# The branch to the general path, moved ahead of the third token tile of the first expert

## The chip, the cores and the metric

The kernel runs on one core of a Trainium2 chip. The core has five engines, each with its own instruction stream: TensorE (PE in the profile, with PEld for its weight loads), VectorE (DVE), ScalarE (ACT), GpSimd (POOL) and SyncE (SP), which here issues most DMAs. They synchronise through semaphores. The metric is the device time of one execution in microseconds.

## The reference

The program is a retention layer (decayed causal attention, 4 batches x 8 heads x 576 positions x 64), then a layer of experts in which each token goes to its best expert alone, then a second layer of experts in which all experts are summed, weighted by a matrix P that is normalised over rows and columns eight times.

```
ret = (q @ k.T / 8) * decay;  x = (ret @ v) as 2304 tokens x 512
logits = x @ w_gate;  expert = argmax(logits);  g = softmax weight of that expert
x = g * (relu(x[expert's tokens] @ w1[expert]) @ w2[expert])        # 8 experts, 512 -> 1024 -> 512
P = exp(x @ w_gate2 - max), normalised 8 times
out = sum over e of P[:, e] * (relu(x @ w1b[e]) @ w2b[e])
```

How many tokens an expert of the first layer gets is known only at run time.

## The kernel before, in words

The retention and the gate go over the 2304 tokens in 18 tiles of 128. The gate counts the tokens of each expert. The first layer of experts is then a list of eight units, sorted by that count, with fixed room for 384, 352, 328, ... tokens (CAPS). Unit 0 takes the expert with the most tokens. If a count does not fit its room, a general path of loops (`anyhow`, L822) does the layer once more for whatever sizes there are. It hangs on one flag, entry [0, 4, 0] of the table `tab`. In the run profiled here the flag is 0, and the general path is jumped over. It has instructions on all five engines, so each of them reads the flag (`nc.values_load`, L829) and takes the branch (`tc.If`, L830) by itself. Where the branch is not taken, each engine does a few semaphore steps in place of what the general path would have counted.

The table `tab` (sorted experts, places, the flag) is worked out on DVE by `final_table` (L602), a generator of small steps. `table_step(n)` (L653) runs up to n of them; the calls are strewn between the matmuls of unit 0, so that the table's steps lie between other DVE work in the program. The step at L644 writes the flag, the one at L648 is the last. L629 writes the token numbers of units 1 to 7, and right behind it `gather(1)` (L665) has POOL issue three indirect DMAs (L671) that fetch unit 1's tokens.

A unit's tokens come as rows and are turned by PE (`gtrans`, L688: four transposes for one tile of 128 tokens); ACT copies the result as a high part HH (L690), DVE makes the low part HL from what is left (L691). Every product is done as three matmuls: high by high, high by low, low by high. Unit 0 is done by `first_unit` (L732), which differs from the others: it takes its three token tiles a = 0, 1, 2 one after another, since the last of them is gathered only when the whole gate is done. For each tile it goes over two halves f of the hidden layer, and for each half over i = 0, 1: `some` issues six matmuls (L697, L698, twice L700 among them). The third tile's transposes, `gtrans(0, 2)`, are issued in tile a = 1, half f = 1, after i = 0. `gemm2` then does the second product of the unit, and the next unit's `gtrans` lie in it. At the end of unit 0, L887 and L888 turn the list of its token numbers into `idsT`, then `anyhow()` stood, then `write(0)`.

The weights are loaded by SP in pieces of 512 KB (`load_more`, L229) into five buffers and split into a high part (ACT, L256) and a low part (DVE and POOL, both L233), which land in a ring of four slots. `keep_up` issues splits between matmuls; a load can go only when the splits of an earlier one are done.

The order of the instructions on an engine is the order in which the code is written: there is no scheduler. What stands in a queue behind an instruction that waits has to wait too.

Of the kernel before, what the change touches and what calls it, by code (L numbers as in the profile page):

```python
# [35 lines left out]
def kernel(  # L36
# [271 lines left out]
    with ExitStack() as at:  # L308
# [228 lines left out]
        def small(n, dt=F32):  # L537
            c = turn.get("s", 0)
            turn["s"] = c + n
            assert c + n <= 1024  # L540
            t = scr[:, c:c + n]
            return t if dt == F32 else t.bitcast(dt)
# [8 lines left out]
        def square(a, b, op):  # L551

            t = cube(E, E)
            nc.vector.tensor_tensor(t, a.unsqueeze(2).to_broadcast([128, E, E]), b.unsqueeze(1).to_broadcast([128, E, E]), op)
            return t
# [10 lines left out]
        def counts():  # L566
            c = small(E)
            nc.vector.tensor_tensor(c, base, cs[:, C_BASE:C_BASE + E], ALU.subtract)
            return c
# [32 lines left out]
        def final_table():  # L602
            turn["s"] = 0
            c = counts()
            key, rank, over, ov = small(E), small(E), small(E), small(1)
            yield
            nc.vector.scalar_tensor_tensor(key, c, 8.0, it8, ALU.mult, ALU.subtract)
            yield
            nc.vector.scalar_tensor_tensor(key, first, 65536.0, key, ALU.mult, ALU.add)
            yield  # L610
            m = square(key, key, ALU.is_lt)
            yield
            nc.vector.tensor_reduce(rank, m, AX.X, ALU.add)
            yield
            m = square(it8, rank, ALU.is_equal)
            yield
            ex = yield from total(m, it8)
            nc.vector.tensor_copy(tab[:, 0, 1:], ex[:, 1:])
            nc.vector.tensor_scalar(tab[:, 1, 1:], ex[:, 1:], float(N), None, ALU.mult)
            n_known[0] = len(raws)  # L620
            load_more()
            yield
            ids = small(3 * E * E).rearrange("p (u a e) -> p u a e", u=E, a=3)
            nc.vector.tensor_tensor(ids, listed[0].rearrange("p e a -> p a e").unsqueeze(1).to_broadcast([128, E, 3, E]),
                                    m.unsqueeze(2).to_broadcast([128, E, 3, E]), ALU.mult)
            yield
            nc.vector.tensor_reduce(rows.rearrange("p (u a) -> p u a", u=E), ids, AX.X, ALU.add)
            yield
            nc.vector.tensor_scalar(allid[:, 3:], rows[:, 3:], float(N), None, ALU.add)  # L629
            gather(1)  # L630
            yield
            cu = yield from total(m, c)
            n = small(E, I32)
            nc.vector.tensor_scalar(n, cu, 127.0, None, ALU.add)
            nc.vector.tensor_tensor(over, cu, cs[:, C_CAP:C_CAP + E], ALU.is_gt)
            yield
            nc.vector.tensor_reduce(ov, over, AX.X, ALU.max)
            nc.vector.tensor_scalar(tab[:, 3], n, 7, None, ALU.arith_shift_right)
            m = square(it8, it8, ALU.is_gt)
            yield  # L640
            r = yield from total(m, cu)
            nc.vector.tensor_tensor(ov, ov, short, ALU.max)
            yield
            nc.vector.tensor_copy(tab[:, 4, 0:1], ov)  # L644
            nc.vector.tensor_scalar(ov, ov, float(N), None, ALU.mult)
            nc.vector.tensor_copy(tab[:, 5], r)
            yield
            nc.vector.tensor_scalar(tab[:, 2], r, ov, None, ALU.max)  # L648
            yield

        table = []

        def table_step(n=5):  # L653
            for _ in range(n):
                if table and next(table[0], 0) == 0:
                    table.pop(0)
# [5 lines left out]
        def tokens(u, a):  # L662
            return min(128, CAPS[u] - 128 * a)

        def gather(u, a0=0, a1=3):  # L665
            if u >= E:
                return
            for a in range(a0, a1):
                n = tokens(u, a)
                x = temp(("p1", "u2", "u3")[a], name="xg")  # L670
                g = nc.gpsimd.indirect_dma_start(  # L671
                    out=x[0:n], out_offset=None, in_=xs[:],
                    in_offset=bass.IndirectOffsetOnAxis(ap=allid[0:n, 3 * u + a:3 * u + a + 1], axis=0),
                )
                arrives(0.73)
                G[u]["x"][a] = x
                if u == 0 and a < 2:
                    ahead.append(g)

        def gtrans(u, a):  # L680
            if u >= E:
                return
            n = tokens(u, a)
            x = G[u]["x"].pop(a)
            tick(0.436)
            p = bank_of("tr", (2, 3)).rearrange("p (k c) -> p k c", k=KB)[:, :, 0:n]
            for r in range(KB):
                nc.tensor.transpose(p[:, r, :], x[0:n, r * 128:(r + 1) * 128], ident[0:n, 0:n])  # L688
            t = slice(a * 128, a * 128 + n)
            nc.scalar.copy(HH[:, :, t], p)  # L690
            nc.vector.tensor_tensor(HL[:, :, t], p, HH[:, :, t].bitcast(F32), ALU.subtract)  # L691
# [40 lines left out]
        def first_unit():  # L732

            hidden(0)
            cc = take(), take()
            hh, hl = G[0]["h"]

            def htrans(a, f, h):
                tick(0.436)
                p = bank_of("tr", (2, 3)).rearrange("p (k c) -> p k c", k=4)  # L740
                for r in range(4):
                    nc.tensor.transpose(p[:, r, :], h[:, r * 128:(r + 1) * 128], ident)
                s, t = slice(f * 4, (f + 1) * 4), slice(a * 128, (a + 1) * 128)
                nc.scalar.copy(hh[:, s, t], p)
                nc.vector.tensor_tensor(hl[:, s, t], p, hh[:, s, t].bitcast(F32), ALU.subtract)

            wait = G[0]["late"] = []

            def late():
                if wait:  # L750
                    htrans(*wait.pop(0))

            for a in range(3):
                if a == 1:
                    gtrans(0, a)
                late()
                t = slice(a * 128, (a + 1) * 128)
                for f, c in enumerate(cc):
                    p = bank_of("h", (0, 1))
                    w = [x.rearrange("p (k f) -> p k f", k=KB) for x in (c.hi, c.lo)]  # L760
                    for i in range(2):
                        some(p, HH[:, :, t], HL[:, :, t], *w, (2 * i, 2 * i + 1), i == 0, i == 1)
                        for _ in range(2):
                            if a:
                                keep_up()
                            table_step(TS)
                        if i == 0:
                            if a == f == 1:
                                gtrans(0, 2)
                            if a > f or a == 2:  # L770
                                late()
                            yield
                    h = temp("c")
                    nc.scalar.activation(h, p, AF.Relu)
                    wait.append((a, f, h))
                    if a == 2:
                        release()
                    yield
            G[0]["late"] = late
# [87 lines left out]
        def unit_steps():  # L867
            for u in range(E):
                n = CAPS[u]
                if u == 0:  # L870
                    yield from first_unit()
                else:
                    gather(u + 1)
                    hidden(u)
                    yield from gemm1(u, 0, n)
                    yield from gemm1(u, 1, n)
                if u == E - 1:
                    return
                for f, d in gemm2(u):
                    if f == 0 and d:  # L880
                        gtrans(u + 1, d - 1)
                    elif u == f == d == 0:
                        G[0]["late"]()
                    yield
                if u == 0:
                    p = bank_of("tr", (2, 3))[0:3 * E, 0:128]
                    nc.tensor.transpose(p, rows, ident)  # L887
                    nc.vector.tensor_scalar(idsT, p, float(N), None, ALU.add)  # L888
                    anyhow()
                write(u)  # L890
                wrote(u)

# [1039 lines left out]
```

## Time and profile before

| what | value |
|---|---|
| median of 3 runs | 1841.89 us (1840.78 to 1845.59) |
| the profiled execution, its own time | 1840.57 us |
| its span, from first to last instruction | 1838.7 us |
| PE busy | 1803.2 us (98%) |
| DVE busy | 1235.5 us (67%) |
| ACT busy | 892.0 us (49%) |
| POOL busy | 567.3 us (31%) |

The profile is one execution on the chip. Busy is the time in which an engine executes; register, branch, semaphore and DMA-issuing instructions do not count as busy and are listed under the engine's queue (PEldq, DVEq, POOLq, SPq). A wait is the idle time of an engine before an instruction, with the one that released it. The change lies in the stretch from about 120 to 170 us, where unit 0 is computed.

### The profile page before, as it was taken

The numbers are of one execution on the slowest core, as the hardware profiler recorded it, in microseconds if no ns is written. First come the engines' busy times: TensorE is split into PE (matmuls) and PEld (weight loads), VectorE is DVE, ScalarE is ACT, GpSimd is POOL, SyncE is SP. The second block draws the span as 40 slices with busy tenths as digits, with TensorE's granted clock in tenths as the row PEclk, the third lists the DMA queues.
The fourth block names the chain that finished last, engine by engine and source line by source line (L and its number), as shares of the span: only waits on it lengthen the run. The fifth ranks groups of instructions, "written<-read, shape, count | busy, mean of one in ns | idle before, by whom it ended". The sixth has DMA issues, their size and how long they took to land.

```text
span 1838.7 us, 32928 instructions
## 1 busy us (share of the span) xinstructions
PE 1803.2 (98%) x12265; PEld 1721.5 (94%) x12265; DVE 1235.5 (67%) x2313; ACT 892.0 (49%) x1718; POOL 567.3 (31%) x582
## 2 busy tenths in 40 slices
PE   8889999999999999999999999999999999999998
PEld 7769999999899999999899999999999999999997
DVE  7984456547645554554467777778877777777778
ACT  2344456544434343434455555555655555555554
POOL 4455577532432323334311112111323111111212
PEclk9999999999999999999999999999999999999999
DMA  8755556564454556444755555655455545555540
GB/s 293 252 174 193 184 185 205 193 204 177 152 215 161 205 173 224 177 178 163 258 158 163 164 158 174 192 155 155 144 173 190 159 155 161 169 155 165 155 127 35
DMA packets 190455, 325.05 MB, mean 177 GB/s; under 512 B 20534, under 2 KB 93383, under 8 KB 190284
## 3 DMA queue, kind: packets, MB, share of 16 engines
q1 hardware_dynamic: 186716, 312.20, 52.0%
q0 software_dynamic: 3136, 9.95, 1.6%
q8 instruction: 99, 1.62, 0.4%
q10 hardware_dynamic: 432, 0.69, 0.1%
q14 instruction: 72, 0.59, 0.1%
HBM read 248.26 MB, written 74.53 MB: 176 GB/s over the span
## 4 chain that ended last, share of the span: by engine, by line
PE 85%; DVE 3%; issue 2%; ACT 1%; POOL 0%; DMA 0%; POOLq 0%; ACTq 0%; DVEq 0%
PE b L1507 8%; PE b L1508 8%; PE b L1509 8%; PE b L1655 8%; PE b L1656 8%; PE b L1654 8%; PE b L1154 5%; PE b L1155 5%; PE b L1156 5%; PE b L1224 4%; PE b L1226 4%; PE b L1225 4%; PE b L705 3%; PE b L706 3%; PE b L707 3%
## 5 line engine op out<-in xcount | busy, mean ns | idle before, releaser
L1655 PE MATMUL b<-wb,sq 128*128 128x256 f32 x1344 | 379.1, 282 | 1.1 <-DVE wb L233 1.1
L1654 PE MATMUL b<-wb,sq 128*128 128x256 f32 x1344 | 378.6, 282 | 0.9 <-DVE a L1676 0.9
L1656 PE MATMUL b<-wb,sq 128*128 128x256 f32 x1344 | 378.9, 282 | 0.4 <-DVE sq L233 0.4
L1655 PEld LDWEIGHTS b<-wb,sq 128*128 128x128 f32 x1344 | 254.7, 190 | 1.7 <-DVE wb L233 1.7
L1654 PEld LDWEIGHTS b<-wb,sq 128*128 128x128 f32 x1344 | 254.5, 189 | 1.8 <-issue 1.3
L1656 PEld LDWEIGHTS b<-wb,sq 128*128 128x128 f32 x1344 | 254.6, 189 | 0.6 <-DVE sq L233 0.6
L233 POOL TENSOR_TENSOR ring<-raw,ring 128x256 fp32r<-128x256 f32 x192 | 172.1, 908 | 262.7 <-ACT ring L256 210.4
L233 DVE TENSOR_TENSOR sq<-hq,sq 128x768 fp32r<-128x768 f32 x167 | 169.9, 1021 | 69.1 <-ACT sq L1600 68.9
L233 DVE TENSOR_TENSOR ring<-raw,ring 128x256 fp32r<-128x256 f32 (+1 forms) x256 | 153.1, 601 | 83.5 <-ACT ring L256 73.8
L1412 POOL TENSOR_TENSOR raw<-raw,raw 128x512 f32<-128x512 f32 x60 | 83.3, 1389 | 387.5 <-DVE wb L233 316.3
L1522 ACT ACTIVATE hq<-hq 128x384 f32<-128x384 f32 x144 | 75.6, 525 | 187.5 <-DVE hq L1519 187.1
L1507 PE MATMUL b<-ch,wa 128*128 128x384 f32 x448 | 152.0, 339 | 2.4 <-DVE hq L1519 0.9
L1224 PE MATMUL b<-ch,ring 128*128 128x384 f32 x448 | 153.2, 342 | 0.1
L1507 PE MATMUL b<-c,wa 128*128 128x384 f32 x448 | 151.6, 338 | 1.0 <-ACT u L1513 1.0
L1600 ACT CAST sq<-hq 128x768 fp32r<-128x768 f32 x167 | 137.7, 830 | 29.7 <-PE b L1655 25.7
L1509 PE MATMUL b<-c,wa 128*128 128x384 f32 x448 | 151.1, 337 | 0.0
L1509 PE MATMUL b<-ch,wa 128*128 128x384 f32 x448 | 151.1, 337 | 0.0
L1508 PE MATMUL b<-cl,wa 128*128 128x384 f32 x448 | 151.0, 337 | 0.0
L1508 PE MATMUL b<-c,wa 128*128 128x384 f32 x448 | 151.0, 337 | 0.0
L1226 PE MATMUL b<-ch,ring 128*128 128x384 f32 x448 | 151.0, 337 | 0.0
L1154 PE MATMUL b<-ring,HH 128*128 128x512 f32 x384 | 150.7, 393 | 0.0
L1225 PE MATMUL b<-cl,ring 128*128 128x384 f32 x448 | 150.6, 336 | 0.0
(257 smaller groups left out, 4359.1 us busy)
## 6 DMA issues: line engine op xcount, KB each, us to landing
wa<-w1s SPq DMA_DIRECT2D x192, 512.0 KB
raw<-in_moe_w_dram SPq DMA_DIRECT2D x128, 512.0 KB
w1s<-ring SPq DMA_DIRECT2D x64, 896.0 KB
raw<-in_moe_w_dram SPq DMA_DIRECT2D x106, 256.0 KB
wa<-w1s SPq DMA_DIRECT2D x64, 256.0 KB
sums<-in_moe_w_dram SPq DMA_DIRECT2D x22, 256.0 KB
kT<-in_kT_dram SPq DMA_DIRECT2D x18, 256.0 KB
qT<-in_qT_dram SPq DMA_DIRECT2D x18, 256.0 KB
```

What stands on the lines that cost most here:

```text
L233: eng.tensor_tensor(lo, x, hi.bitcast(F32), ALU.subtract)
L1154: nc.tensor.matmul(y[t], hh[:, s], w.hi[:, f0:f0 + 512], start=first, stop=False)
L1224: nc.tensor.matmul(ps, a, xh[:, r, :], start=first and r == 0, stop=False, skip_group_check=True)
L1225: nc.tensor.matmul(ps, a, xl[:, r, :], start=False, stop=False, skip_group_check=True)
L1226: nc.tensor.matmul(ps, b, xh[:, r, :], start=False, stop=r == 1, skip_group_check=True)
L1507: nc.tensor.matmul(ps, a, xh[:, r, :], start=first, stop=False, skip_group_check=True)
L1508: nc.tensor.matmul(ps, a, xl_[:, r, :], start=False, stop=False, skip_group_check=True)
L1509: nc.tensor.matmul(ps, b, xh[:, r, :], start=False, stop=r == 1, skip_group_check=True)
L1600: nc.scalar.copy(o.tile[0], src.tile)
L1654: nc.tensor.matmul(ps, hh[:, r, c], wh[:, r], start=st, stop=False, skip_group_check=True)
L1655: nc.tensor.matmul(ps, hh[:, r, c], wl[:, r], start=False, stop=False, skip_group_check=True)
L1656: nc.tensor.matmul(ps, hl[:, r, c], wh[:, r], start=False, stop=kh == 1 and r == 1, skip_group_check=True)
```

## The change

Three lines of code move. In `first_unit`, in tile a = 1, half f = 1, after i = 0, ahead of the third tile's transposes: all steps of the table that are left are issued at once (`table_step(99)`), then the general path with its branch (`anyhow()`). `gather(1)` leaves the table and is issued behind the transposes. At the end of unit 0 `anyhow()` is gone.

```
@@ final_table
             nc.vector.tensor_scalar(allid[:, 3:], rows[:, 3:], float(N), None, ALU.add)
-            gather(1)
             yield
@@ first_unit
                         if i == 0:
                             if a == f == 1:
+                                table_step(99)
+                                assert not table
+                                anyhow()
                                 gtrans(0, 2)
+                                gather(1)
                             if a > f or a == 2:
                                 late()
                             yield
@@ unit_steps
                     nc.vector.tensor_scalar(idsT, p, float(N), None, ALU.add)
-                    anyhow()
                 write(u)
```

The code behind it shifts by a few lines: L688 to L691 are L687 to L690 after, L829 and L830 are L833 and L834.

On PE, in unit 0, the third tile's transposes (L688; `xg` is the gathered tile, `ring` the split weights) stand between the matmuls of tile 1. Before:

```order
L697 MATMUL b_2243<-ring_79,HH 128x512
L698 MATMUL b_2243<-ring_79,HH 128x512
L700 MATMUL b_2243<-ring_79,HL 128x512 x2
L688 MATMUL b_2259<-cs,xg 128x128 x4
L697 MATMUL b_2243<-ring_79,HH 128x512
L698 MATMUL b_2243<-ring_79,HH 128x512
```

Now the load of the flag (L833) and the branch (L834) stand ahead of them, and the general path's 208 rows between the branch and its end:

```order
L696 MATMUL b_2237<-ring_79,HH 128x512
L697 MATMUL b_2237<-ring_79,HH 128x512
L699 MATMUL b_2237<-ring_79,HL 128x512 x2
L833 TENSOR_LOAD tab
L834 COMPARE_AND_BRANCH
...
L834 UNCONDITIONAL_BRANCH
L687 MATMUL b_3658<-cs,xg 128x128 x4
L696 MATMUL b_2237<-ring_79,HH 128x512
```

The transposes and all of the rest of unit 0 have moved behind the branch; what stood ahead of them is the same. The transposes write a bank of PSUM that the general path uses too, and in the new order they wait for a count of DVE that DVE reaches behind its own branch.

On DVE, the last steps of the table stood on both sides of the third tile's low part (L691). Before:

```order
L554 TENSOR_TENSOR sums<-cs 128x64
L560 TENSOR_TENSOR sums<-sums 128x64
L562 TENSOR_REDUCE sums<-sums 128x8
L691 TENSOR_TENSOR HL<-b_2259,HH 128x4x128
L642 TENSOR_TENSOR sums<-sums,short 128x1
L644 CAST tab<-sums 128x1
L645 TENSOR_SCALAR sums<-sums 128x1
L646 CAST tab<-sums 128x8
L648 TENSOR_SCALAR tab<-sums 128x8
```

Now they follow each other, and the branch stands behind them:

```order
L554 TENSOR_TENSOR sums<-cs 128x64
L560 TENSOR_TENSOR sums<-sums 128x64
L562 TENSOR_REDUCE sums<-sums 128x8
L641 TENSOR_TENSOR sums<-sums,short 128x1
L643 CAST tab<-sums 128x1
L644 TENSOR_SCALAR sums<-sums 128x1
L645 CAST tab<-sums 128x8
L647 TENSOR_SCALAR tab<-sums 128x8
L833 TENSOR_LOAD tab
L834 COMPARE_AND_BRANCH
```

Five small instructions have moved up by one place; L691 comes behind the branch.

On POOL, the gathers for unit 1 stood between two weight splits. Before:

```order
L233 TENSOR_TENSOR ring_71<-raw_65,ring_71 128x256 x2
L671 DMA xg<-xs,allid 128x512 x2
L671 DMA xg<-xs,allid 96x512
L233 TENSOR_TENSOR ring_78<-raw_66,ring_78 128x256 x2
```

Now POOL's branch stands ahead of them:

```order
L233 TENSOR_TENSOR ring_71<-raw_65,ring_71 128x256 x2
L833 TENSOR_LOAD tab
L834 COMPARE_AND_BRANCH
...
L834 UNCONDITIONAL_BRANCH
L670 DMA xg<-xs,allid 128x512 x2
L670 DMA xg<-xs,allid 96x512
L233 TENSOR_TENSOR ring_78<-raw_66,ring_78 128x256 x2
```

The gathers keep their place among the splits; the branch, six pairs of splits earlier than before, comes ahead of them. On SP six of the weight loads that stood ahead of the branch stand behind it, and on ACT the casts from the third tile's L690 on.

## Rows read from the trace of the kernel before

**Rows 1.** Page, busy time of an engine (share of the span) and instructions.
```profile
PE 1803.2 (98%) x12265; PEld 1721.5 (94%) x12265; DVE 1235.5 (67%) x2313; ACT 892.0 (49%) x1718; POOL 567.3 (31%) x582
```
**Rows 2.** Stretches: length; busy of PE, PEld, DVE, ACT, POOL; clock, DMA share, GB/s.
```profile
127.07:128.74 1.67, 0.00 (x1) 0.03 (x1) 1.67 (x3) 0.22 (x1) 1.67 (x3) 1.00 0.36 135
132.11:133.97 1.86, 0.00 (x1) 0.00 (x0) 1.72 (x10) 0.00 (x0) 1.55 (x2) 1.00 0.90 330
158.35:159.88 1.53, 0.01 (x1) 0.03 (x1) 0.28 (x1) 0.41 (x1) 0.00 (x0) 1.00 0.28 94
```
**Rows 3.** Timeline of PE: start, duration, instruction, [wait before it, its releaser].
```profile
126.45 0.61 PE L700 MATMUL b<-ring,HL 128*128 128x512 f32 x2
128.74 0.63 PE L688 MATMUL b<-cs,xg 128*128 128x128 f32 x4 [1.67 <-DMA xg<-xs,allid]
...
133.97 0.73 PE L700 MATMUL b<-ring,HL 128*128 128x512 f32 x2 [1.86 <-DVE sums L642]
...
144.32 0.60 PE L688 MATMUL b<-cs,xg 128*128 128x128 f32 x4
...
159.88 0.40 PE L705 MATMUL b<-HH,ring 128*128 128x352 f32 x1 [1.53 <-PEq L830]
```
**Rows 4.** Timeline of DVE, the table's last steps.
```profile
133.10 0.22 DVE L562 TENSOR_REDUCE sums<-sums 128x8 f32<-128x64 f32 x1
133.24 0.68 DVE L691 TENSOR_TENSOR HL<-b,HH 128x512 fp32r<-128x512 f32 x1
133.84 0.15 DVE L642 TENSOR_TENSOR sums<-sums,short 128x1 f32<-128x1 f32 x1
134.02 0.15 DVE L644 CAST tab<-sums 128x1 int32<-128x1 f32 x1
```
**Rows 5.** Line L829, the flag's load: ns min/median/max, first and last start (us).
```profile
L829 PEldq TENSOR_LOAD <-tab x1: 483/483/483, 155.2 to 155.2; - x1
...
L829 DVEq TENSOR_LOAD <-tab x1: 546/546/546, 158.4 to 158.4; - x1
```
**Rows 6.** Line L830, branch and semaphore steps behind it; SP's in two stretches.
```profile
L830 POOLq EVENT_SEMAPHORE  x5: 17/43/43, 160.4 to 160.7; - x5
...
L830 DVEq EVENT_SEMAPHORE  x2: 21/21/21, 163.3 to 163.4; - x2
L830 PEldq COMPARE_BRANCH  x1: 3826/3826/3826, 155.7 to 155.7; - x1
L830 POOLq COMPARE_BRANCH  x1: 58/58/58, 157.8 to 157.8; - x1
...
L830 DVEq COMPARE_BRANCH  x1: 72/72/72, 159.0 to 159.0; - x1
...
L830 SPq EVENT_SEMAPHORE  x5: 17/17/17, 163.6 to 163.9; - x5
...
L830 SPq EVENT_SEMAPHORE  x4: 17/17/17, 166.6 to 166.9; - x4
```
**Rows 7.** Stretches: the branch's new place, and DVE's jump before.
```profile
134.20:138.50 4.30, 4.30 (x24) 3.55 (x24) 2.34 (x7) 2.31 (x5) 1.64 (x3) 1.00 0.89 322
159.00:163.30 4.30, 3.42 (x21) 3.45 (x22) 0.00 (x0) 0.00 (x0) 1.04 (x2) 1.00 0.38 133
```
**Rows 8.** Stretches: a thin one of PE in the retention, and the next.
```profile
81.50:84.90 3.40, 1.55 (x21) 1.22 (x18) 3.08 (x15) 2.25 (x6) 0.90 (x3) 1.00 0.39 146
84.90:88.30 3.40, 3.40 (x35) 2.92 (x34) 2.74 (x11) 0.30 (x2) 2.66 (x3) 0.50 0.96 277
```
**Rows 9.** Timeline of POOL; last, gathers of L671 from issue to landing.
```profile
132.01 0.97 POOL L671 DMA_INDIRECT xg<-xs,allid  x1 [0.31 <-DVE sums L560]
133.29 0.95 POOL L671 DMA_INDIRECT xg<-xs,allid  x1 [0.31 <-issue]
...
137.82 4.58 POOL L233 TENSOR_TENSOR ring<-raw,ring 128x256 fp32r<-128x256 f32 x5 [2.35 <-ACT ring L256]
...
DMA to landing us min/median/max: 3.4/5.6/8.5
```

More of the change, by code (lines that the diff above doesn't have):

```diff
@@ L629, in final_table @@
             nc.vector.tensor_scalar(allid[:, 3:], rows[:, 3:], float(N), None, ALU.add)
-            gather(1)
             yield
@@ L768, in first_unit @@
                             if a == f == 1:
+                                table_step(99)
+                                assert not table
+                                anyhow()
                                 gtrans(0, 2)
+                                gather(1)
                             if a > f or a == 2:
@@ L888, in unit_steps @@
                     nc.vector.tensor_scalar(idsT, p, float(N), None, ALU.add)
-                    anyhow()
                 write(u)
```

## The prediction

> **What bounds the kernel now.** I read first the busy time of the engines: TensorE (PE) is busy 1803.2 us of the 1838.7 us span [rows 1], so only its idle time can be lost or won, and a change of order is worth what it does to PE's waits. Then I looked for PE's waits in the stretch that the diff touches, 127 to 160 us. The busy time by stretch shows three in which PE does nothing: 1.67 us, 1.86 us and 1.53 us, 5.06 us together [rows 2]. The timeline of PE says what ends each [rows 3]. At 128.74 the transposes of the third token tile (L688) start when the gathered rows have landed. At 133.97 the first matmul with the low part HL starts, which VectorE (DVE) wrote late (L691 ends at 133.92 [rows 4]; the row names DVE's next step). At 159.88 PE comes out of the branch to the general path (PEq L830). Nothing else in this stretch idles PE. The timeline of DVE then explains the second wait and dates the flag on which the branch decides: DVE is at work on weight splits and on the table; its last table steps are L562 at 133.10, then the tile's HL (L691) at 133.24, then L642 at 133.84 and L644 at 134.02, which writes the flag and takes 0.15 us [rows 4]. Last I read the flag's load and the branch engine by engine [rows 5, 6].
>
> **The change, part by part.** *The table in one go.* Five DVE steps (L642 to L648) move ahead of one, L691. L642 takes the place of L691 at 133.24, and L644 follows 0.18 us later, so the flag stands at 133.24 + 0.18 + 0.15 = 133.57 us, 0.6 us earlier than before [rows 4]. It can't be much earlier, since all other table steps stood ahead of L691 already, and nothing that DVE does between 127 and 133 us waits for PE.
>
> *The branch, on PE.* It moves from the end of the unit to a place that PE reaches at 127.07 us (the last matmul before it starts at 126.45 [rows 3]; its wait starts at 127.07 [rows 2]). There PE must wait for the flag, read it, jump, and only then do the transposes. In the trace PE's sequencer reads the flag at 155.2 and the first matmul behind the branch starts at 159.88: 4.68 us, of which the jump itself is 3.83 and the rest 0.85 [rows 3, 5, 6]. The array lost only 1.53 us of this, because the sequencer was some 3 us ahead of it: work queued before the branch still ran until 158.35, when the array's wait starts [rows 2]. This cover is gone in the new place: the sequencer stands at the flag while the array runs dry.
>
> *How long a jump takes there.* After its compare-and-branch at 159.0 DVE goes on at 163.3, 4.3 us later; POOL needed 2.6 us (157.8 to 160.4) [rows 6]. There PE jumped at 155.7, POOL at 157.8, DVE at 159.0; now all five engines are released by one write and jump together, and in that stretch the DMA engines carry 322 GB/s at a share of 0.89, against 133 GB/s at 0.38 while DVE jumped [rows 7]. So for PE: 3.83 us if company costs nothing, 3.83 + (4.3 - 2.6) = 5.5 us if it costs PE what it cost DVE beside POOL. I take 5.0, nearer to the upper end because more engines and more traffic meet. PE goes on at 133.57 + 0.85 + 5.0 = 139.4 us. A second leg reaches the same place: the transposes behind the branch write a bank that the general path uses too, so they wait for DVE to be through its own branch; from flag to the end of its jump DVE needs 5.0 us (158.4 to 163.4 [rows 5, 6]), 138.6 us here. Even a cheap jump of PE would thus not be used.
>
> *Sum of the waits.* New wait: 139.4 - 127.07 = 12.3 us. What it replaces: the landing of the gather (long over by 139), the wait for HL (DVE has nothing else to do by then, L691 takes 0.68 us [rows 4], and PE needs HL only 133.97 - 1.86 - 128.74 = 3.4 us after the transposes start), and the old branch: 5.06 us. Net +7.3 us. The bounds: +4.9, if both legs jump in POOL's 2.6 us (PE goes on at 137.0), and +10.0, if one of them stands still a second time as SP did (2.7 us, under the rivals).
>
> *The clock.* In the trace PE waited 1.67 and 1.86 us here and its granted clock stayed full, 2.4 GHz [rows 2]. But at 81.5 to 84.9 us, where it was busy 1.55 of 3.4 us, the granted clock of the next 3.4 us was 0.50, the lower level of 1.2 GHz [rows 8]. A wait of 12 us is emptier than either, so I expect the lower level when PE goes on, for a stretch like that one: 3.4 us at half speed cost 1.7 us. Bounds: 0, as after the short waits, and 3.4, two such stretches. The Trainium skill ("TensorE: Matmul & The Clock Gate", Part 1: The HAM clock gate) holds that half speed is the resting state and only activity lifts it. By this rule the 1.7 us are due; by the row of the 1.86 us wait nothing would be, and the sum would end at 1847.9. I side with the rule because the rows at 81.5 us do.
>
> *What moves past POOL and SP.* The three gathers for the next unit now stand behind POOL's branch. Before they began at 132.01 [rows 9]; now POOL is through at about 138 to 139, issues them 1.3 us apart, and the longest landing is 8.5 us [rows 9], so the first is in by 149. PE needs it 144.32 - 128.74 - 1.86 = 13.7 us after it goes on [rows 3], at 153. Hidden, with 4 us to spare. POOL's weight splits, the first at 137.82 before [rows 9], are due 137.82 - 1.86 - 128.74 = 7.2 us after PE goes on, at 146.6; POOL is free at 143. Six weight loads move behind SP's branch; each waits for splits of that kind, so they lose nothing. ScalarE's (ACT's) casts fall back with PE. I cost all this at 0; if the cover failed, a late gather would cost up to 1 or 2 us.
>
> Sum, against the profiled execution's own 1840.57 us (1.9 us more than its span): +7.3 + 1.7 = +9.0, 1849.6 us. The median of the three runs shown is 1841.89, 1.3 us above the profiled one, the best of them 1840.78; I predict 1850.0.
>
> **The rivals.** *A hidden jump (the other side: not slower).* While PE stands at the flag it could have the target's code at hand; then it goes on at 133.57 + 0.85 = 134.4, the wait is 7.4 us, and the kernel takes 1840.6 + 2.3 = 1842.9, no change. For it: the array paid only 1.53 us for the old branch [rows 2]. Against it: that was queued work, and DVE, with nothing queued, stood still for 4.3 us [rows 6]; DVE's leg must be short too. It decides below a jump of about 3.2 us, where the loss falls under 5.5 us. For a gain, PE would have to go on before 127.07 + 5.06 = 132.1, ahead of the flag itself. The Trainium skill ("Runtime: NRT & Kernel Launch", Instruction fetch mechanics) says that a jump out of the code already fetched waits for a DMA. By this rule the hidden jump falls away; no row shows an engine that stood waiting ahead of its branch.
>
> *A second fetch.* Behind its jump SP did five semaphore steps from 163.6 to 163.9 and the other four from 166.6 [rows 6]: it stood still again for 2.7 us. If PE's new place, or DVE's or ScalarE's that PE needs next, has such a break, add 2.7: 1849.6 + 2.7 = 1852.3, and with a longer stretch at half clock about 1853.5. Nothing in the trace tells which engine it hits; it hit one of five.
>
> *The clock stays up.* Sum without 1.7: 1847.9 with my jump, 1846.7 with PE's 3.83.
>
> **How the numbers follow.** The forecast has 0.57 (own range 1848 to 1852.5), the second fetch 0.20, the clock that stays 0.12, the hidden jump 0.11. A measurement of this kernel tells about 0.3%, 5.5 us, from no change. Slower by more: the forecast, the second fetch and about half of the third, 0.84. Within: the other half and most of the hidden jump, 0.14. Faster: 0.02. The range takes the bounds of the sum: 1840.57 + 4.9 = 1845.5 below, and above 1840.57 + 10.0 + 3.4 + 1.3 = 1855.3, rounded to 1855.5; it leaves the hidden jump out.
>
> **What would show it.** Right: one wait of PE of about 12 us from 127 us, ended by the branch, no wait for HL and none at the unit's end, a granted clock of 0.5 behind it; DVE's flag write ending near 133.6; everything behind shifted alike. Wrong: PE going on before 137, the flag much earlier or later, the clock at full, or a new wait for the gather at the next unit's first transposes.

## The result, and the profile after

| | median | lowest to highest | runs |
|---|---|---|---|
| before | 1841.93 us | 1840.78 to 1845.59 | 4 |
| after | 1852.18 us | 1851.43 to 1853.67 | 4 |

The ratio is 1.0053, 95% interval 1.0038 to 1.0068: 10.25 us slower, which is more than the 5.5 us that can be told from no change. The forecast was 1850.0 us, its range 1845.5 to 1855.5. The profiled execution after took 1852.76 us, its span 1851.0 us, 12.3 us more than before's span.

The page's busy times are those of [rows 1] but for a few us; the loss is idle time of PE.

```profile
PE 1806.0 (98%) x12265; PEld 1724.6 (93%) x12265; DVE 1236.3 (67%) x2313; ACT 892.2 (48%) x1718; POOL 566.0 (31%) x582
```

The timeline of PE answers to [rows 3] (start, duration, instruction, wait before it with its releaser):

```profile
128.89 0.61 PE L699 MATMUL b<-ring,HL 128*128 128x512 f32 x2
143.91 1.09 PE L687 MATMUL b<-cs,xg 128*128 128x128 f32 x4 [14.41 <-PEq L834]
...
160.07 0.60 PE L687 MATMUL b<-cs,xg 128*128 128x128 f32 x4
...
173.83 0.27 PE L891 MATMUL b<-cs,rows 128*24 128x128 f32 x1
173.86 0.41 PE L704 MATMUL b<-HH,ring 128*128 128x352 f32 x1
```

Three waits have become one of 14.41 us ahead of the third tile's transposes, ended by the branch. The wait for HL is gone, the next unit's transposes at 160.07 wait for nothing, and at the unit's end (173.86) PE goes straight on. By stretches (columns as in [rows 2]), the wait as a whole, two parts of it, and what comes behind it:

```profile
129.51:143.91 14.40, 0.00 (x0) 0.03 (x1) 6.35 (x23) 0.21 (x1) 4.99 (x7) 0.61 0.63 204
136.40:141.00 4.60, 0.00 (x0) 0.00 (x0) 0.00 (x0) 0.00 (x0) 0.00 (x0) 0.50 0.90 309
...
143.91:149.70 5.79, 5.79 (x18) 4.81 (x19) 1.32 (x2) 1.77 (x3) 2.84 (x3) 0.50 0.34 97
149.70:153.00 3.30, 3.30 (x17) 2.73 (x17) 0.76 (x2) 1.20 (x3) 0.00 (x0) 1.00 0.21 63
98.50:101.90 3.40, 3.40 (x21) 2.77 (x16) 2.61 (x9) 1.12 (x3) 2.11 (x3) 0.50 0.73 218
```

DVE works 6.35 us of the 14.40 and then stops. From 136.40 to 141.00 no engine computes, while the DMA engines are busy at a share of 0.90 (0.81 over the 7.03 us of PE's jump, dated below). Behind the wait the granted clock is 0.50 for 5.79 us, then 1.00 again. (The last row is a stretch of the retention, for the accounts below.) DVE's timeline dates the flag, as [rows 4] did:

```profile
135.30 0.22 DVE L562 TENSOR_REDUCE sums<-sums 128x8 f32<-128x64 f32 x1
135.44 0.15 DVE L641 TENSOR_TENSOR sums<-sums,short 128x1 f32<-128x1 f32 x1
135.62 0.15 DVE L643 CAST tab<-sums 128x1 int32<-128x1 f32 x1
...
145.66 0.69 DVE L690 TENSOR_TENSOR HL<-b,HH 128x512 fp32r<-128x512 f32 x1 [9.42 <-ACT HH L689]
```

Then the flag's load and the branch, engine by engine (ns min/median/max, first to last start), as [rows 5, 6]:

```profile
L833 PEldq TENSOR_LOAD <-tab x1: 491/491/491, 135.8 to 135.8; - x1
L834 SPq EVENT_SEMAPHORE  x9: 17/17/17, 143.8 to 144.4; - x9
L834 POOLq EVENT_SEMAPHORE  x5: 17/42/43, 144.0 to 144.3; - x5
L834 DVEq EVENT_SEMAPHORE  x2: 21/21/21, 143.6 to 143.8; - x2
L834 POOLq COMPARE_BRANCH  x1: 58/58/58, 136.4 to 136.4; - x1
L834 PEldq COMPARE_BRANCH  x1: 7033/7033/7033, 136.4 to 136.4; - x1
L834 DVEq COMPARE_BRANCH  x1: 72/72/72, 136.6 to 136.6; - x1
```

The flag stands at 135.62 + 0.15 = 135.77. PE jumps at 136.4 for 7.03 us; POOL goes on at 144.0 (7.6 us) and DVE at 143.6 (7.0). The five jump together and are through together. Last, the DMA queues while they jump, 136.4 to 143.5 us (packets, MB, share of 16 engines), and SP's issues:

```profile
q1 hardware_dynamic: 924, 1.77, 78.0%
q14 instruction: 4, 0.03, 1.3%
q8 instruction: 1, 0.02, 0.9%
```

```profile
132.78 2.90 SPq L229 DMA_DIRECT2D raw<-in_moe_w_dram  x5
```

Five weight loads of 512 KB, issued up to 0.7 us before the branch, fill the DMA engines, and the few packets of instructions share these engines with them. PE's code comes as one packet of 16 KB on q8: before's trace has one at 157.12, the only instruction packet between PE's branch at 155.7 and POOL's at 157.8. After has it at 141.06, 4.6 us behind PE's branch, and PE is through 2.4 us later. The DMA view of 141.0 to 141.5 us:

```profile
q8 instruction: 1, 0.02, 13.0%
```

**Where the 12.3 us went.** I paired the matmuls of the two traces by their place in the program. After is 2.45 us late already where it reaches the place (129.51 against 127.07). In this execution the retention has one more stretch at half clock, from 98.5, beside that of [rows 8]; about 1.1 us came with it, 1.0 us had gathered in small steps before it, and the rest came behind it. The code of the retention is the same in both, so I put the 2.45 us down to the scatter of executions and not to the change. Then, in us: +12.74 for the wait (14.41 in place of 1.67), +2.6 for the half clock behind it, -1.92 for the wait for HL, -1.87 for the old branch, -0.42 just behind that, -1.25 for several small waits later. Sum 12.3; without the retention's part 9.9, against 10.25 between the medians.

### The profile page after: what moved, and what is told of

The parts are those of the page before. It is cut to its first block, busy times and chain, and to the rows that moved or that the text cites. A ratio compares the mean times of both kernels' runs of the same rounds, so it can differ in the third digit from the quotient of the medians.

```text
span 1851.0 us, 32923 instructions
## 1 busy us (share of the span) xinstructions
PE 1806.0 (98%) x12265; PEld 1724.6 (93%) x12265; DVE 1236.3 (67%) x2313; ACT 892.2 (48%) x1718; POOL 566.0 (31%) x582
## 4 chain that ended last, share of the span: by engine, by line
PE 86%; DVE 2%; issue 2%; ACT 1%; DMA 0%; POOL 0%; POOLq 0%; ACTq 0%; DVEq 0%
PE b L1510 8%; PE b L1511 8%; PE b L1512 8%; PE b L1658 8%; PE b L1659 8%; PE b L1657 8%; PE b L1157 5%; PE b L1158 5%; PE b L1159 5%; PE b L1227 4%; PE b L1229 4%; PE b L1228 4%; PE b L704 4%; PE b L706 4%; PE b L705 4%
```

## The experiments

Two theories of the 7 us jump. T, traffic: the code that an engine jumps to comes by DMA, and comes late because it stands among five weight loads. C, company: five engines fetch at once, and that costs. Each run is compared with the kernel before on the same chip (median 1843.42 us for e1 to e4, 1843.14 us for e5 to e8).

**e1: the loads behind the branch.** After, with the five loads taken out of the table and issued behind the branch.

```
@@ final_table
-            n_known[0] = len(raws)
-            load_more()
             yield
@@ first_unit
                                 anyhow()
+                                n_known[0] = len(raws)
+                                load_more()
                                 gtrans(0, 2)
```

> The changed kernel, with one thing more: the five weight loads that the table releases (and their order to SP) are issued behind the branch instead of ahead of it, so that nothing else moves on the DMA engines while the five engines jump. Theory T (the fetch of the code behind the jump stands in line behind the weight loads): PE's jump falls from 7.0 us to between 2.6 and 4.3 us, the wait at the third tile from 14.4 to about 11 us, the other engines' jumps likewise; the time falls by about 3 us against the changed kernel, to some 1849 us. Theory C (five fetches at once are slow, whatever else moves): the jump stays at 7 us and the time at 1852 us. Under both the clock is at half behind the wait.

Measured: 1849.36 us, ratio 1.0033 (1.0021 to 1.0044). The branch, the timeline of PE, and two stretches of e1:

```profile
L834 POOLq EVENT_SEMAPHORE  x5: 17/42/43, 138.1 to 138.4; - x5
...
L834 DVEq EVENT_SEMAPHORE  x2: 21/21/21, 138.5 to 138.6; - x2
L834 POOLq COMPARE_BRANCH  x1: 58/58/58, 134.4 to 134.4; - x1
L834 PEldq COMPARE_BRANCH  x1: 3373/3373/3373, 134.4 to 134.4; - x1
L834 DVEq COMPARE_BRANCH  x1: 72/72/72, 134.7 to 134.7; - x1
```

```profile
138.64 1.09 PE L685 MATMUL b<-cs,xg 128*128 128x128 f32 x4 [11.38 <-DVEq L834]
```

```profile
134.40:138.50 4.10, 0.00 (x0) 0.00 (x0) 0.00 (x0) 0.00 (x0) 0.00 (x0) 0.50 0.05 12
138.64:143.20 4.56, 4.56 (x15) 3.87 (x16) 0.69 (x1) 1.21 (x3) 2.83 (x3) 0.50 0.48 155
```

All five engines still jump together, at a DMA share of 0.05 instead of 0.90, and PE's jump is 3.37 us instead of 7.03. So T holds for PE, and C falls for PE: in e4 and e8 below, where the engines jump one after another, its jump takes 3.37 and 3.49 us. Company is not free for every engine: POOL's jump takes 3.7 us here (134.4 to 138.1) and took 2.6 in the old place [rows 6], and SP's takes 3.9 here and 2.5 to 2.6 in e4 and e8, where it is the first to jump. Why stays open. PE's packet now starts 1.0 us behind its branch, and PE is again through 2.4 us later. The DMA view of e1, 135.0 to 135.5 us:

```profile
q8 instruction: 1, 0.02, 12.5%
```

It took as long as after's (1.00 against 1.04 us). What the loads lengthen is therefore the time until the packet starts. With the DMA share over PE's jump, it is 1.0 us in e1, e2, e4 and e8 (0.05 to 0.11), 1.4 to 1.7 in before, e5 and e7 (0.33 to 0.44), 3.5 in e3 (0.88), and 4.6 and 4.8 in after and e6 (0.81 and 0.87). In all of them PE is through 2.4 to 2.7 us after the packet's start.

PE is through its own branch at 137.8, but goes on at 138.64, when DVE is through its: the second leg of the prediction, seen on its own. The wait is 3.0 us shorter than after's; the half clock stays. The interval of the ratio overlaps with after's, so the 3 us are read from the wait and not from the times.

**e2: a filler ahead of the branch.** e1, with 40 matmuls of no use queued on PE ahead of the flag's load, so that PE is busy while it would wait.

```
                                 table_step(99)
                                 assert not table
+                                fp = bank(7)
+                                for _ in range(40):
+                                    nc.tensor.matmul(fp, HH[:, 0, 0:128], w[0][:, 0], start=True, stop=True)
                                 anyhow()
```

> As the kernel before it in this list (loads behind the branch), with 40 matmuls of 512 columns into a bank that nobody reads, ahead of the branch on PE: 9.3 us of array work that lies inside the wait. Theory 'the clock falls because the array is empty': under T the empty time left is about 2 us, the granted clock stays at 1.0 and the 2.6 us that the half clock cost behind the wait are gone, time some 2.6 us under the kernel without the matmuls. Rival (the matmuls hold up the flag's load, since PE's sequencer has to get past them): PE goes on later by up to 3 us, and nothing is gained.

Measured: 1847.27 us, ratio 1.0023 (1.0013 to 1.0033). Timeline of PE and the stretch behind the branch in e2:

```profile
127.76 9.23 PE L771 MATMUL b<-ring,HH 128*128 128x512 f32 x40
139.35 0.63 PE L685 MATMUL b<-cs,xg 128*128 128x128 f32 x4 [2.37 <-DVEq L837]
```

```profile
139.35:144.00 4.65, 4.65 (x27) 3.95 (x28) 1.38 (x2) 2.00 (x4) 2.84 (x3) 1.00 0.46 151
```

PE reaches the place at 127.76 and goes on 11.6 us later, as late as in e1 (11.4), so the filler stands in nobody's way. The clock stays at 1.00, and in 4.65 us PE does 27 instructions where e1 did 15 in 4.56. At e2's pace those 15 take 4.65 * 15 / 27 = 2.6 us, so e1 lost about 2 us; its median is 2.1 us longer. That the clock falls behind this wait because PE is idle, and what it costs, is thereby shown, though the intervals of the two ratios overlap.

**e3: traffic at the old place.** Before, with four loads of 384 KB that nobody reads, issued as unit 0 ends.

```
+                    if u == 0 and f == d == 1:
+                        for j, tg in enumerate(("x00", "x01", "x10", "x11")):
+                            junk = xc_p.tile([128, 2, 384], F32, tag=tg, name="junk")
...
+                            nc.sync.dma_start(out=junk, in_=w21[j][0:256, 0:384].rearrange("(k p) f -> p k f", p=128))
```

> The kernel before, branch in its old place, with four loads of 384 KB into buffers that nobody uses yet, issued from about 155 us on, so that the DMA engines are busy while PE jumps (each engine still jumps at its own time as before). Theory T: PE's jump grows from 3.8 us to 6 or 7, its wait at the unit's end from 1.5 to 4 or 5 us, time +3 us. Theory C: PE's jump stays at 3.8 us, its wait at 1.5 us, time as before.

Measured: 1844.58 us, ratio 1.0003 (0.9994 to 1.0013). The branch, PE's timeline and stretches of e3:

```profile
L830 PEldq COMPARE_BRANCH  x1: 5932/5932/5932, 157.0 to 157.0; - x1
```

```profile
163.24 0.63 PE L705 MATMUL b<-HH,ring 128*128 128x352 f32 x1 [3.64 <-PEq L830]
```

```profile
157.00:163.00 6.00, 2.60 (x16) 2.25 (x14) 0.75 (x3) 1.48 (x3) 1.62 (x2) 0.94 0.88 253
163.24:169.00 5.76, 5.76 (x20) 5.76 (x21) 1.36 (x3) 1.59 (x3) 2.10 (x2) 0.50 0.66 215
```

PE jumps alone here, 2.1 us ahead of the next engine, and still takes 5.93 us at a DMA share of 0.88; undisturbed it took 3.83 [rows 6], and 4.23 and 4.31 in e5 and e7, which leave the old branch alone. This shows T from the other side. The wait grows from 1.53 to 3.64 us, less than the 4 to 5 that I expected, and in this execution half clock follows. The 3 us that I expected in the time did not come: 1.2 us more in the medians can't be told from nothing, and the interval ends at 2.4 us.

**e4 and e8: the flag known.** The branch in its new place hangs on a constant 0, so the general path is left out. The table's steps, with the next unit's gathers and the five loads among them, are held until the branch is issued and run behind it. In e4 the constant is a new tile, in e8 it lies in a cell that existed.

```
...
-            flag = nc.values_load(tab[0:1, 4, 0:1], min_val=0, max_val=1)
+            flag = nc.values_load(zero[0:1, 0:1], min_val=0, max_val=1)                  # e4
+            flag = nc.values_load(gap.bitcast(I32)[0:1, 0:1], min_val=0, max_val=1)      # e8
```

> The branch in its new place, but it hangs on a constant 0 written at the start, and the table's steps, with the next unit's gathers in them, run behind the branch. It leaves out that the general path is taken when counts don't fit. Theory (of the 14.4 us, 6.3 are the wait for the flag and 7 the jump, lengthened by the loads that the table releases): no engine waits for the flag, no load is in flight, the engines jump at 124 to 128 us in 2.6 to 4.3 us each, and PE's wait at the third tile is 2 to 5 us instead of 14.4; the waits for HL and at the unit's end are gone; time 1840 to 1843 us. Rival: the later table makes the next unit's gathers late (they are needed 13.7 us behind the transposes), and 2 to 5 us come back there: 1844 to 1846 us.

> Once more the branch in its new place on a constant 0, table and gathers behind it, but the constant lies in a cell that the kernel has already, so that no buffer moves to another address. It leaves out that the general path is taken when counts don't fit. In the run with a cell of its own, PE lost 5 us evenly between 440 and 1600 us, far from the change. Theory (that loss came with the new cell, not with the branch): it is gone, PE's wait at the third tile is about 5 us again, ended by DVE's branch, the waits for HL and at the unit's end are gone, time 1842 to 1844 us. Rival (the loss belongs to the branch or to chance): 1847 us or more again.

Measured: e4 1847.99 us, ratio 1.0029 (1.0018 to 1.004); e8 1841.74 us, ratio 0.9995 (0.9986 to 1.0004). e4's PE waits 4.64 us in the new place, e8's 3.98. Branch and PE's timeline in e8:

```profile
L835 DVEq EVENT_SEMAPHORE  x2: 21/21/21, 135.8 to 135.9; - x2
...
L835 PEldq COMPARE_BRANCH  x1: 3493/3493/3493, 128.7 to 128.7; - x1
...
L835 DVEq COMPARE_BRANCH  x1: 72/72/72, 132.3 to 132.3; - x1
```

```profile
135.88 1.09 PE L690 MATMUL b<-cs,xg 128*128 128x128 f32 x4 [3.98 <-DVEq L835]
```

```profile
135.88:141.90 6.02, 6.02 (x19) 4.95 (x20) 2.60 (x10) 1.77 (x3) 0.85 (x2) 0.50 0.01 3
```

PE's jump is over at 132.2, nearly all of it hidden behind work that was queued ahead of the branch, yet PE goes on at 135.88 because DVE jumps from 132.3 to 135.8. This cover is that of the old branch and not the hidden jump of the rivals, which was to come from code at hand. DVE's leg takes most of it back, and half clock follows the wait here too. Still, one wait of 4 us in place of three of 5.06 makes no measurable difference in the times. In e8 the flag is not late, and the five loads are not in flight: the two together make the loss, not the place alone, and e1 gives the loads' share, 3.0 us of the wait.

e4 missed its expected 1840 to 1843 by 5 us, and its wait does not explain them. Paired by matmuls, e4 falls behind by 5.2 us between 440 and 1600 us, where the code is the same: there the new 4-byte tile had moved the buffers behind it by 32 bytes (HH from 58720 to 58752). The same 7225 matmuls, far behind the change, in before, in e4 and in e8:

```profile
440.19:1600.04 1159.85, 1156.00 (x7225) 1111.34 (x7224) 776.07 (x1238) 572.30 (x1078) 293.29 (x288) 1.00 0.54 176
```

```profile
445.84:1610.89 1165.05, 1161.94 (x7225) 1115.87 (x7224) 774.32 (x1238) 572.69 (x1078) 293.42 (x289) 1.00 0.54 175
```

```profile
445.73:1605.00 1159.27, 1155.56 (x7225) 1111.21 (x7224) 774.25 (x1238) 572.30 (x1078) 294.11 (x289) 1.00 0.54 176
```

At full clock e4 takes 1165.05 us for them where before takes 1159.85, and e8, with the addresses kept, 1159.27. The loss is uneven: from 400 to 1800 us the mean time from one matmul to the next goes from 228.95 to 233.08 ns at before's L1155 (512 columns) and from 118.91 to 120.10 at L1655 (256 columns), while L1654, of the same shape as L1655, loses nothing. That the shift costs is shown by this pair alone; why it does stays open.

**e5: the table alone.** Before, with the table completed ahead of the third tile's transposes and the branch left at the unit's end.

```
                             if a == f == 1:
+                                table_step(99)
+                                assert not table
                                 gtrans(0, 2)
```

> The kernel before with one part of the change alone: all table steps that are left are issued ahead of the third tile's transposes (the branch stays at the unit's end). Theory: five small DVE steps come ahead of the tile's low part HL, which ends 0.6 us later; PE's wait for it grows from 1.9 to 2.4 us, the other two waits stay, time +0.5 us, no change that can be measured. Rival (the table in one go takes part in the loss): +2 us or more.

Measured: 1843.78 us, ratio 1.0005 (0.9996 to 1.0014). PE's timeline and one stretch of e5:

```profile
129.52 0.63 PE L688 MATMUL b<-cs,xg 128*128 128x128 f32 x4 [1.98 <-DMA xg<-xs,allid]
...
134.93 0.73 PE L700 MATMUL b<-ring,HL 128*128 128x512 f32 x2 [0.44 <-DVE HL L691]
```

```profile
130.20:133.60 3.40, 3.40 (x11) 2.74 (x10) 3.16 (x14) 1.34 (x3) 3.24 (x5) 0.50 0.44 148
```

The longer wait for HL that I expected did not come, for a poor reason: in this execution a wait of 1.98 us was followed by half clock, and the slower PE needed HL later. What follows holds for the medians: the table's order alone costs nothing measurable.

**e6: two of the gathers ahead of the branch.** After, with two of unit 1's three gathers back in the table.

```
@@ final_table
+            gather(1, 0, 2)
             yield
@@ first_unit
-                                gather(1)
+                                gather(1, 2, 3)
```

> The changed kernel with two of the next unit's three gathers back in the table, ahead of POOL's branch (the third needs a buffer that is free only behind the transposes). Theory: the gathers' place costs nothing, since they are needed some 15 us later; PE's wait stays at 14 us, time as the changed kernel, 1852 us. Rival (POOL's late branch or the gathers' own transfers hold up the others): the wait grows to 16 us or more.

Measured: 1851.61 us, ratio 1.0049 (1.0035 to 1.0064), not to be told from after's 1.0053. PE's branch and its wait in e6:

```profile
L835 PEldq COMPARE_BRANCH  x1: 7273/7273/7273, 134.2 to 134.2; - x1
```

```profile
142.37 1.09 PE L688 MATMUL b<-cs,xg 128*128 128x128 f32 x4 [15.18 <-DVEq L835]
```

The gathers' place is worth nothing in the time, as costed, and the long jump is there a second time, with the same five loads in flight. The wait is 15.18 us, 0.8 more than after's 14.41 and less than the rival's 16, since DVE, through only at 142.2, ends it.

**e7: the table's tail held back.** Before, with the table's last steps held until the third tile is under way, to see whether the wait for HL can be had for nothing.

```
+            while held[0]:
+                yield
             cu = yield from total(m, c)
...
                     if a == 2:
+                        held[0] = False
                         release()
```

> The kernel before, branch in its old place, the other way round from the change: the table's steps behind the next unit's gathers (seven yields, L560 to the flag) are held until the third tile, so that DVE makes the third tile's HL 1.6 us earlier. Theory: PE's wait for HL falls from 1.9 to 0.3 us, the flag is still written 15 us ahead of the branch, the other waits stay: 1.5 us less than before. Rival (something else ends last at that place, or the steps push later splits back): no gain. The times may not tell 1.5 us; the wait in the profile will.

Measured: 1844.36 us, ratio 1.0008 (0.9998 to 1.0017). PE's timeline of e7:

```profile
143.20 0.44 PE L709 MATMUL b<-h,ring 128*128 128x384 f32 x1 [2.31 <-DVE h L748]
```

The wait for HL is gone, and one of 2.31 us has come in its place, since the same DVE steps now delay the tile's hidden layer. No version that was run and computes everything beats the kernel before.

## Why the prediction was right, point by point

- *The flag* was put 6.50 us behind the moment at which PE runs dry, and came 135.77 - 129.51 = 6.26 us behind it. Right.
- *The jump* is the term that was mis-sized most: 5.0 us forecast, within 3.83 to 5.5, and 7.03 measured. The step that failed, in a forecast that came out within its range, is "3.83 us if company costs nothing, 3.83 + (4.3 - 2.6) = 5.5 us if it costs PE what it cost DVE beside POOL". It took company for the price and weighed the traffic only as a reason to stay near the upper end, though the DMA share of 0.89 stood in [rows 7]. The runs show the reverse: in the new place, 3.37 us (e1, e4), 3.43 (e2) and 3.49 (e8) on quiet DMA engines, 7.03 (after) and 7.27 (e6) among the loads. Asked of that row, the question "whose transfers are these, and does the fetch stand among them?" would have put a jump of more than 5.5 us among the bounds.
- *The rest* around the jump: 0.85 forecast, 0.63 from flag to jump plus 0.48 behind it measured.
- *The new wait*: 12.3 forecast, 6.26 + 0.63 + 7.03 + 0.48 = 14.40 measured.
- *DVE's leg* ("Even a cheap jump of PE would thus not be used"): right, shown by e1, e2, e4, e6 and e8, where DVE's branch ends PE's wait.
- *What is replaced*: 5.06 us forecast; all three waits are gone, and with them 1.67 + 1.92 + 1.87 = 5.46 us. Another 0.42 + 1.25 us of small waits went that I had not counted; that work behind a long wait finds DVE and the loads ahead of it would explain them, but no run tests it.
- *The clock*: that it falls was right, e2 shows it; 1.7 us were put on it, 2.6 were lost. I took the length of the stretch from [rows 8], 3.4 us, and here it was 5.79.
- *Gathers, loads and casts* behind the branch at 0: right. The gathers were issued from 145.50, and the transposes at 160.07 do not wait; e6 moves two of them without effect.
- *The rivals*: the second fetch did not occur, SP's nine semaphore steps run from 143.8 to 144.4 without a break; its 1852.3 was hit by another cause. The clock did not stay up. The hidden jump fell: PE stood at the flag, and its jump took 7.03 us, and 3.37 in e1 on quiet DMA engines. The sum of this rival and its limit of 3.2 us left the clock out, though by the forecast's own argument a wait of 7.4 us would have lowered it too; in e8 a wait of 3.98 us was followed by half clock.

Jump, rest and clock together were 3.2 us short, and against them stand 0.2 us of the flag, 0.4 of the waits replaced and 1.7 of the small ones: 9.0 + 3.2 - 2.3 = 9.9, what the pairing found without the retention's part. So the mechanism was right but for the price of the jump, and that the time came out within 2.2 us of the forecast is in part luck: errors that partly cancel, not a right jump.

The Trainium skill ("Runtime: NRT & Kernel Launch", Instruction fetch mechanics) says that a jump out of the code already fetched waits for a DMA. The runs agree: each jump of PE has its packet on q8 and takes 3.37 us at the least. They add that this packet starts late where the kernel's own loads fill the DMA engines, 4.6 us behind the branch in after.

## What to carry to other kernels

A branch on a late value cost PE three things here: the wait for the value, a fetch of code, and a slower clock once it had run dry. Put such a branch where work is still queued ahead of it, so that PE's sequencer can do all this while the array is busy. Before costing a jump, look at what the DMA engines carry in that stretch, and keep bulk loads behind the branch if it must stand there. And look for the other engines' branches: PE pays for the last of those on whose counts it waits.

## What was not expected

- A jump of PE took 3.4 us with the DMA engines at 0.05, and 7.0 to 7.3 us with them at 0.81 to 0.87; PE's jump beside four others took no longer than where the engines jumped one after another. The fetch itself was no slower among the loads, it started later.
- Half clock followed a wait of only 1.98 us in e5, where a wait of 1.86 us was followed by full clock in before [rows 2, 3] and one of 2.01 us in e7.
- A shift of buffers by 32 bytes slowed matmuls that nothing else touched, those of one line from 228.95 to 233.08 ns each, 5 us in all.
- How many stretches at half clock the retention has differs between executions of the same retention code (before's profile shows one, after's two, e8's three, e1's none). That this makes part of the scatter of before's times, 1840 to 1847 us, is likely but not shown.
